# 512-column matmuls in place of 128-column ones in the idle stretches of TensorE

## The chip, the core and the metric

The kernel runs on one core of a Trainium2 chip. Its engines work side by side, each on its own list of instructions in order: TensorE (PE; its weight loads are listed apart, as PEld), VectorE (DVE), ScalarE (ACT), GpSimd (POOL) and SyncE (SP), which here only starts transfers. They wait for one another by semaphores. The metric is the device time of one execution in microseconds (us); of the kernel before it is 308.48 us, the median of three runs (307.95 to 309.0).

## The reference

Attention over selected chunks, then a gated feed-forward layer on its result, cut to what matters:

```python
B, H, S, D = 4, 8, 768, 64;  chunk, top_k = 32, 6
k_min, k_max = min and max of k over each chunk of 32 tokens
ub   = sum_d max(q * k_min, q * k_max)            # a bound for each query and chunk
ub   = where(causal by chunk, ub, -1e9)
sel  = the 6 chunks with the largest ub
attn = softmax(where(sel & causal, q @ k.T / sqrt(D), -1e9)) @ v
x    = attn, heads side by side                   # 3072 tokens x 512
xn   = x / sqrt(mean(x*x) + 1e-6) * rms_g
g    = xn @ w_gate                                # 512 -> 1536
out  = (silu(g) * (xn @ w_val)) @ w_out           # 1536 -> 512
```

Inputs and output are float32.

## The kernel before, in words

**Tiling.** The 768 tokens of each of the 4 batch entries are cut into 3 blocks of 256, 12 blocks in all, worked through in the list `ORDER`. A block has two groups `g` of four heads. For every block and group, `job` turns k and q so that the head's dimension lies on the partitions (DVE, L639), makes bfloat16 copies `kb` and `qb` (L646/L647), takes the chunks' minimum and maximum `kx` (DVE, L654) and lays them out in `BD`. `pick` multiplies them with q in float32 on PE (`upper`, L559), finds the sixth largest bound with DVE (`ubn`, `bar`, `top`, `mk`, `mt`, L580 to L611) and so makes the masks `mtd` and `mto`. Then come the scores with the masks added on PE (L717, L728), the exponential on ACT (L767), the causal triangle on POOL (L737), the product with v on PE (`values`, L793), and the division on DVE (L812). `norm` takes the root mean square (ACT, POOL), and turns the rows with PE (`turn`, L856).

`ffn` takes 512 columns of a gate product `wg` and of a value product `wv` in PSUM (16 matmuls of 128 columns each, or 8 of 256; L894), a tanh on ACT (L901), `tg` on DVE (L905), a copy `vs` of the value product on ACT (L913) and the product `hh` on POOL (L916); for the pairs in `DIRECT` the product is taken on DVE from PSUM (L909) and there is no copy. Then 24 matmuls of 512 columns (`project`, L926) for each 128 tokens, a copy out and a store. The first two blocks are in `SPLIT`: their feed-forward part runs in halves of 128 tokens, and part of their scores needs no mask.

**Weights.** `wg`, `wv` and `wo` are loaded in three thirds each, in nine transfers of 512 KB issued by POOL from 10.3 us on (wg0, wv0, wg1, wv1, wg2, wv2, wo0, wo1, wo2). A gate product of the second third of the hidden columns needs wg1 and wv1. By `HELD`, the k and v of the third block wait for wg0 and wv0, and those of the fourth for wo0.

**Order.** The whole order is laid down ahead by `Plan.run` when the program is built: each operation has an assumed duration, a priority `pri` (lower goes first), the operations it needs, and the buffers it takes. The planner picks, time step by time step, for each engine the operation that can start. Priorities come from due times: `due_ffn(i) = PACE * i` and `due_attn(i) = PACE * i - LEAD`. `MARGIN` is time that it adds to the expected landing of later loads. The chip doesn't follow the assumed times; it keeps the order on each engine, and the semaphores do the rest.

**Filler.** `fill` tells the planner what to do where PE would be idle for a while in its own times, from 1.6 to 60 us: it puts in matmuls whose result nobody reads (`keep_busy`, L991), into a free PSUM buffer `F`. Up to `cold` = 5.6 it reckons with twice `step` for each, after that with `step` = 0.0565 us:

```python
n = int(max(0.0, min(t1, cold) - t0) / (2 * step) + max(0.0, t1 - max(t0, cold)) / step)
...
TE.matmul(store["F"][slot][:, 0:P], ident[:], ident[:], start=True, stop=True)
```

Each of them is a weight load and a matmul in PE's list. There are 256 of them, all within the first 40 us.

Of the kernel before, what the change touches and what calls it, by code (L numbers as in the profile page):

```python
# [10 lines left out]
ALU = mybir.AluOpType  # L11
ACT = mybir.ActivationFunctionType
# [102 lines left out]
class Plan:  # L115
# [44 lines left out]
    def run(self, in_order=(), fill=None):  # L160
        left = {k: len(v) for k, v in self.readers.items()}
        last = {}
        slot = self.slot = {}
        head = {p: 0 for p in self.fifo}
        at = {e: 0.0 for e in self.HOP}
# [57 lines left out]
        while todo:  # L223
            best = None
            for e, c in cand.items():
                if not c:
                    continue
                rows = [(est(o, e), o) for o in c]
                rows = [(t, o) for t, o in rows if t is not None]
                if not rows:  # L230
                    continue
                t0 = max(at[e], min(t for t, o in rows))
                now = sorted(((t, o) for t, o in rows if t <= t0 + 1e-9),
                             key=lambda r: (r[1].pri, r[1].seq))
                t, o = now[0]
                if e in self.PATIENT:
                    soon = [r for r in rows if r[0] <= t0 + self.PATIENT[e]]
                    for t, o in now + sorted(soon, key=lambda r: (r[1].pri, r[1].seq)):
                        end = t + o.alts[e][0] - 0.1
                        if not any(t < r[0] < end and r[1].pri < o.pri - 10 for r in soon):  # L240
                            break
                    t0 = max(t0, t)
                if best is None or (t0, o.pri) < (best[0], best[1].pri):
                    best = (t0, o, e)
            if best is None:
                stuck = [o.name for c in cand.values() for o in c][:12]
                raise RuntimeError(f"no op can go on: {stuck}")
            t, o, e = best
            todo -= 1
            if e == "PE" and fill is not None:  # L250
                begin, cold, end, step, pool, fn = fill
                t0 = max(begin, at[e])
                f = sorted(x for x in self.free[pool] if x[0] + 0.055 <= t0)
                t1 = min(t, end) - (0.11 if o.mode != "full" else 0.03)
                n = int(max(0.0, min(t1, cold) - t0) / (2 * step) + max(0.0, t1 - max(t0, cold)) / step)
                if n > 0 and f:
                    w = Op("warm", "PE", t1 - t0, t1 - t0, lambda n=n, x=f[0][1]: fn(n, x), 0)
                    w.seq, w.start, w.mode = -1, t0, "full"
                    w.done = at[e] = t1
                    mode = "full"  # L260
                    order.append(w)
            for x in o.alts:
                cand[x].remove(o)
            o.eng = e
            o.occ, o.lat, o.fn = o.alts[e]
            if e == "PE" and mode is not None and mode != o.mode:
                t += 0.105
            if e == "PE":
                mode = o.mode
            o.start = t  # L270
            if e in port and shares(o, e):
                port[e] = (t, t + o.lat - 0.06)
            at[e] = t + o.occ
            o.done = t + o.lat
            if o.dma is not None:
                packets, cost, hw = o.dma
                rings.add(max(2.3, t + o.occ + (0.6 if hw else 1.4)), e, packets, cost, o)
                if hw:
                    at[e] = max(at[e], rings.room(e, t))
                if hw:  # L280
                    lanes.append(o)
            for key in o.takes:
                p = self.pool_of[key]
                if p in strict:
                    while head[p] < len(self.fifo[p]) and self.fifo[p][head[p]].start is not None:
                        head[p] += 1
                self.free[p].sort()
                slot[key] = self.free[p].pop(0)[1]
            for key in o.uses:
                last[key] = max(last.get(key, 0.0), o.done)  # L290
                left[key] -= 1
                if not left[key]:
                    self.free[self.pool_of[key]].append((last[key], slot[key]))
            order.append(o)
            for u in o.users:
                n_dep[u.seq] -= 1
                if not n_dep[u.seq]:
                    offer(u)
# [6 lines left out]
def kernel(  # L305
# [12 lines left out]
    P = nc.NUM_PARTITIONS  # L318
# [11 lines left out]
    NHT = DFF // P  # L330
    NTOK = B * S
    SCALE = 1.0 / (D ** 0.5)
    KH = NHT // 2
# [13 lines left out]
    def at(key):  # L347
        return store[plan.pool_of[key]][plan.slot[key]]
# [46 lines left out]
    ORDER = [(0, 0), (1, 0), (2, 0), (3, 0), (0, 1), (1, 1), (0, 2), (2, 1), (1, 2),  # L395
             (3, 1), (2, 2), (3, 2)]
    assert sorted(ORDER) == [(b, m) for b in range(B) for m in range(NBLK)]
    PACE, LEAD = 23.0, 70
    MARGIN = 3.0
    FIRST = 8  # L400
    SPLIT = {0, 1}
    APART = set()
    PACKED = {0, 1, 2}
    DIRECT = {(i, hp) for i in range(len(ORDER)) for hp in range(KH) if i >= 4 and hp % 2}

    def HALVES(i):
        return ((0,), (1,)) if i in SPLIT else ((0, 1),)
# [1 line left out]
    def due_attn(i):  # L409
        return PACE * i - LEAD  # L410
# [465 lines left out]
    def ffn(i, toks):  # L876
# [7 lines left out]
        for hp in range(KH):  # L884
            third = 3 * hp // KH
            gp, vp = ("gp", *U, hp), ("vp", *U, hp)
            th, vs, tg, hh = ("th", *U, hp), ("vs", *U, hp), ("tg", *U, hp), ("hh", *U, hp)
            pri = base + hp * 6 // KH
            for nm, p_, w in (("wg", gp, wg), ("wv", vp, wv)):
                def gate(p_=p_, w=w, hp=hp):  # L890
                    for n in range(K):
                        ht = K * hp + n
                        for g in range(NP):
                            TE.matmul(at(p_)[:, n * W:(n + 1) * W],  # L894
                                      w[:, g, ht * P:(ht + 1) * P], at(xT)[:, g, 0:W],
                                      start=(g == 0), stop=(g == NP - 1), skip_group_check=True)

                o = plan.op(f"{nm}{U}.{hp}", "PE", 0.873, 1.035, gate, pri,
                            reads=[xT, (nm, third)], writes=[p_], takes=[(p_, "F")])
                o.mode = "full"  # L900
            plan.op(f"tanh{U}.{hp}", "ACT", 0.48, 0.6, lambda th=th, gp=gp: SE.activation(  # L901
                out=at(th), in_=at(gp), func=ACT.Tanh, scale=0.5), pri - 20, reads=[gp], writes=[th],
                takes=[(th, "th")])
            plan.op(f"tg{U}.{hp}", "DVE", 0.6, 0.69, lambda th=th, gp=gp, tg=tg:
                    VE.scalar_tensor_tensor(  # L905
                        out=at(tg), in0=at(th), scalar=1.0, in1=at(gp), op0=ALU.add,
                        op1=ALU.mult), pri - 30, reads=[th, gp], writes=[tg], takes=[(tg, "tg")])
            if (i, hp) in DIRECT:
                plan.op(f"hh{U}.{hp}", "DVE", 0.6, 0.69, lambda tg=tg, vp=vp, hh=hh: VE.tensor_tensor(  # L909
                    out=at(hh), in0=at(tg), in1=at(vp), op=ALU.mult), pri - 30, reads=[tg, vp],  # L910
                    writes=[hh], takes=[(hh, "hh")])
                continue
            plan.op(f"vcopy{U}.{hp}", "ACT", 0.48, 0.6, lambda vs=vs, vp=vp: SE.activation(  # L913
                out=at(vs), in_=at(vp), func=ACT.Copy), pri + 0.1, reads=[vp],
                writes=[vs], takes=[(vs, "vs")])
            plan.op(f"hh{U}.{hp}", "POOL", 1.11, 1.16, lambda tg=tg, vs=vs, hh=hh: GE.tensor_tensor(  # L916
                out=at(hh), in0=at(tg), in1=at(vs), op=ALU.mult), pri - 10, reads=[tg, vs],
                writes=[hh], takes=[(hh, "hh")])
        for k_, s in enumerate(toks):
            op, ob = ("op", i, s), ("osb", i, s)  # L920
# [2 lines left out]
            def project(h0, h1, k_=k_, op=op):  # L923
                for ht in range(h0, h1):
# [8 lines left out]
                        writes=[op], takes=[(op, "F")])  # L933
            o.mode = "full"
            o = plan.op(f"project{i}.{s}+", "PE", 0.216 * K, 0.216 * K + 0.17,
                        lambda project=project: project(last, NHT), pri - 10,
                        reads=[("hh", *U, KH - 1), op], writes=[op])
            o.mode = "full"
            flex(f"out{i}.{s}", {
# [20 lines left out]
    for i in range(len(ORDER)):  # L960
# [12 lines left out]
            for j in jobs:  # L973
                next(j, None)
        for toks in HALVES(i):
            norm(i, toks, due_attn(i) + (7 if toks[-1] else -3))
        if i == 0:
            for n in range(3):
                load_w(n, -290 if n == 0 else -36 + n)
# [6 lines left out]
        for toks in HALVES(i):  # L986
            ffn(i, toks)

    def keep_busy(n, slot):
        for _ in range(n):  # L990
            TE.matmul(store["F"][slot][:, 0:P], ident[:], ident[:], start=True, stop=True)  # L991

    for o in plan.run(in_order=("kraw", "qraw", "vraw", "kT", "qT", "kb", "qb", "VX", "xsT", "xs", "hh", "xnat"),
                      fill=(1.6, 5.6, 60.0, 0.0565, "F", keep_busy)):
        o.fn()
    kernel.plan = plan
# [28 lines left out]
```

The softmax here doesn't subtract the row's maximum and nothing guards it: scores larger than these inputs give would overflow.

## Time and profile before

| | before |
|---|---|
| time, median of 3 | 308.48 us |
| span of the profiled execution | 307.3 us |
| PE busy from 0 to 8, 8 to 24, 24 to 50 us | 6.55 of 8, 15.16 of 16, 23.80 of 26 us |
| PE busy from 50 to 303 us | 249.29 of 253 us |
| fillers (L991) | 256, 20.03 us, the last at 39.2 us |
| mean granted TensorE clock | 0.987 |
| instructions fetched for PE (queue q8) | 39 packets, 0.64 MB |

Landing of the weights' last piece, by the trace's semaphore updates: wg0 18.91, wv0 21.45, wg1 25.45, wv1 29.70, wg2 33.10, wv2 36.42, wo0 39.82, wo1 42.86, wo2 46.37 us.

How to read it: an engine's busy time is the sum of its instructions in the stretch; the rest is idle. The granted clock is the share of full speed that the throttle let TensorE have. In the profile's chain of waits each piece of the span is put down to the instruction that the end waited for, and "issue" to time for which the records name no releaser. A group line gives source line, engine, operation and what it writes and reads. Queue q8 carries instructions only; q0 the weights; q1 and q10 the other loads and the stores.

### The profile page before, as it was taken

The numbers are of one execution on the slowest core, as the hardware profiler recorded it, in microseconds if no ns is written. First come the engines' busy times: TensorE is split into PE (matmuls) and PEld (weight loads), VectorE is DVE, ScalarE is ACT, GpSimd is POOL, SyncE is SP. The second block draws the span as 40 slices with busy tenths as digits, with TensorE's granted clock in tenths as the row PEclk, the third lists the DMA queues.
The fourth block names the chain that finished last, engine by engine and source line by source line (L and its number), as shares of the span: only waits on it lengthen the run. The fifth ranks groups of instructions, "written<-read, shape, count | busy, mean of one in ns | idle before, by whom it ended". The sixth has DMA issues, their size and how long they took to land.

```text
span 307.3 us, 11903 instructions
## 1 busy us (share of the span) xinstructions
PE 294.8 (96%) x4966; PEld 233.1 (76%) x4992; DVE 218.3 (71%) x560; ACT 210.4 (68%) x364; POOL 146.6 (48%) x266
## 2 busy tenths in 40 slices
PE   8897999998999999999999999999999999999994
PEld 8796999666867867876885876788588598688671
DVE  7994498865896898999999898269467245247250
ACT  3663786778986996966788777669478479565240
POOL 4783488656773694553656553235243034114130
PEclk9997899999999999999999999999999999999999
DMA  8999995575853434555763500100110010010101
GB/s 191 239 213 254 197 207 124 131 191 136 212 120 105 108 68 114 131 132 129 166 132 103 140 3 2 70 5 0 36 38 2 2 71 3 35 38 0 69 2 68
DMA packets 74838, 30.66 MB, mean 100 GB/s; under 512 B 65568, under 2 KB 70176, under 8 KB 74784
## 3 DMA queue, kind: packets, MB, share of 16 engines
q1 hardware_dynamic: 69184, 24.66, 32.9%
q0 software_dynamic: 4752, 4.72, 9.1%
q8 instruction: 39, 0.64, 0.9%
q10 hardware_dynamic: 848, 0.53, 0.6%
q14 instruction: 15, 0.12, 0.1%
HBM read 28.31 MB, written 6.29 MB: 113 GB/s over the span
## 4 chain that ended last, share of the span: by engine, by line
PE 88%; DVE 3%; issue 2%; ACT 2%; DMA 1%; POOL 1%; ACTq 0%; DVEq 0%
PE F L894 40%; PE F L926 19%; PE S L717 8%; PE F L793 7%; PE S L559 6%; PE F L991 3%; PE S L728 3%; PE F L856 2%; DMA qraw<-in_q_dram 1%; DVE kx L654 1%; DVE qT L639 1%; DVE tg L905 0%; POOL pt L737 0%; ACT junk L828 0%; ACT th L901 0%
## 5 line engine op out<-in xcount | busy, mean ns | idle before, releaser
L767 ACT ACTIVATE pt<-S 128x1024 bf16<-128x1024 f32 (+3 forms) x104 | 86.2, 861 | 23.5 <-PE S L728 23.0
L916 POOL TENSOR_TENSOR hh<-tg,vs 128x512 bf16<-128x512 bf16 x48 | 55.9, 1168 | 64.8 <-ACT vs L913 42.8
L894 PE MATMUL F<-xsT,wg 128*128 128x256 bf16 (+1 forms) x672 | 75.7, 260 | 0.5 <-DVE xnat L812 0.4
L894 PE MATMUL F<-xsT,wv 128*128 128x256 bf16 (+1 forms) x672 | 74.7, 257 | 0.0
L905 DVE SCALAR_TENSOR_TENSOR tg<-th,F 128x512 bf16<-128x512 bf16 x72 | 48.7, 680 | 35.8 <-ACT th L901 34.6
L926 PE MATMUL F<-wo,hh 128*128 128x512 bf16 x262 | 63.8, 379 | 1.9 <-issue 1.0
L894 PEld LDWEIGHTS <-wg 128*128 128x128 bf16 x672 | 57.4, 99 | 8.3 <-issue 0.9
L894 PEld LDWEIGHTS <-wv 128*128 128x128 bf16 x672 | 57.2, 98 | 7.5 <-issue 0.3
L901 ACT ACTIVATE th<-F 128x512 bf16<-128x512 f32 x72 | 43.0, 599 | 20.3 <-PE F L894 17.8
L737 POOL TENSOR_SCALAR_AFFINE_SELECT pt<-pt 128x512 bf16<-128x512 bf16 x48 | 31.1, 654 | 37.6 <-ACT pt L767 36.5
L926 PEld LDWEIGHTS <-hh 128*128 128x128 bf16 x288 | 26.4, 98 | 28.0
L913 ACT ACTIVATE vs<-F 128x512 bf16<-128x512 f32 x48 | 28.4, 600 | 9.3 <-PE F L894 8.4
L717 PE MATMUL S<-qb,kb 32*128 32x256 bf16 (+1 forms) x800 | 33.1, 254 | 0.7 <-DVE ubn L580 0.3
L654 DVE TENSOR_REDUCE kx<-kT 128x16 f32<-128x512 f32 x48 | 30.0, 668 | 0.0
L793 PE MATMUL F<-VX,pt 128*128 128x65 bf16 x672 | 27.1, 194 | 0.9 <-POOL kx L659 0.7
L793 PEld LDWEIGHTS <-pt 128*128 128x128 bf16 x672 | 24.1, 98 | 3.0 <-issue 1.4
L828 ACT ACTIVATE junk<-xnat 128x512 bf16<-128x512 bf16 x24 | 15.2, 633 | 13.1 <-DVE xnat L812 8.2
L717 PEld LDWEIGHTS <-kb 32*128 32x128 bf16 x800 | 13.8, 93 | 13.0 <-issue 11.9
L991 PE MATMUL F<-ident 128*128 128x128 bf16 x256 | 20.0, 244 | 1.9 <-POOL ident masks.py:199 1.4
L812 DVE TENSOR_TENSOR xnat<-F,rden 128x256 bf16<-128x256 f32 x48 | 20.1, 423 | 1.3
L728 PE MATMUL S<-mtd,chunkrow 32*128 32x128 bf16 (+2 forms) x384 | 20.5, 203 | 0.0
L728 PE MATMUL S<-mto,chunkrow 32*128 32x128 bf16 (+2 forms) x384 | 19.9, 203 | 0.0
(60 smaller groups left out, 357.3 us busy)
## 6 DMA issues: line engine op xcount, KB each, us to landing
vraw<-in_v_dram SPq DMA_DIRECT2D x24, 256.0 KB, 4.4
out_dram<-osb SPq DMA_DIRECT2D x24, 256.0 KB, 2.2
kraw<-in_k_dram SPq DMA_DIRECT2D x72, 64.0 KB, 2.5
qraw<-in_q_dram SPq DMA_DIRECT2D x72, 64.0 KB, 2.2
wg<-in_moe_w_gate_dram POOLq DMA_DIRECT2D x3, 512.0 KB, 12.3
wv<-in_moe_w_val_dram POOLq DMA_DIRECT2D x3, 512.0 KB, 15.8
wo<-in_moe_w_out_dram POOLq DMA_DIRECT2D x3, 512.0 KB, 22.7
kraw<-in_k_dram SPq DMA_DIRECT2D x10, 128.0 KB, 4.3
```

Source lines behind the costliest of these rows:

```text
L654: plan.op(f"ext{n}{J}", "DVE", 0.585, 0.67, lambda n=n, op=op: VE.tensor_reduce(out=at(kx)[:, n], in_=at(kT).rearrange("p h (c t) -> p h c ...
L717: TE.matmul(s[a // 2][:, a % 2, c0:c0 + q1 - q0], kbt[r, t, ks], qbt[r, t, q0:q1], start=(t == 0), stop=(t == 1 and not mask), skip_group_ ...
L728: TE.matmul(o, chunkrow[r, BLK * kg + P * e:BLK * kg + P * (e + 1)], mv, start=False, stop=(d == 1), skip_group_check=True)
L737: GE.affine_select(out=d, in_=d, compare_op=ALU.is_ge, fill=0.0, base=0, pattern=[[0, 4], [1, P]], channel_multiplier=-1)
L767: lambda pt=pt, hs=hs, c0=c0, c1=c1, x=sc[hp]: SE.activation(out=at(pt)[:, hs, c0:c1], in_=at(x)[:, :, c0:c1], func=ACT.Exp, scale=SCALE), ...
L793: TE.matmul(o[:, a, :], p_[:, a, off:off + P], vt[:, e, a, :], start=(kb_ == 0 and a == 0), stop=(kb_ == nkb - 1 and a == 3), skip_group_c ...
L894: TE.matmul(at(p_)[:, n * W:(n + 1) * W], w[:, g, ht * P:(ht + 1) * P], at(xT)[:, g, 0:W], start=(g == 0), stop=(g == NP - 1), skip_group_ ...
L901: plan.op(f"tanh{U}.{hp}", "ACT", 0.48, 0.6, lambda th=th, gp=gp: SE.activation(out=at(th), in_=at(gp), func=ACT.Tanh, scale=0.5), pri - 2 ...
L905: VE.scalar_tensor_tensor(out=at(tg), in0=at(th), scalar=1.0, in1=at(gp), op0=ALU.add, op1=ALU.mult), pri - 30, reads=[th, gp], writes=[tg ...
L916: plan.op(f"hh{U}.{hp}", "POOL", 1.11, 1.16, lambda tg=tg, vs=vs, hh=hh: GE.tensor_tensor(out=at(hh), in0=at(tg), in1=at(vs), op=ALU.mult) ...
L926: TE.matmul(at(op)[:], at(("hh", *U, ht // K))[:, o:o + P], wo[:, ht, :], start=(ht == 0), stop=(ht == NHT - 1))
L991: TE.matmul(store["F"][slot][:, 0:P], ident[:], ident[:], start=True, stop=True)
```

## The change

From 5.6 us of the planner's time on, a gap on PE is filled with matmuls of 512 columns (the moving operand is 512 columns of `chunkrow`), one for each 0.216 us of the gap, in place of one of 128 columns for each 0.0565 us. Before 5.6 us the filler stays as it was. The same work time then takes a quarter of the instructions. With it, constants of the planner are set anew: `PACE`, `LEAD`, `MARGIN`, the set `APART` (blocks in which the choice of chunks is done for one group of heads after the other), the set `DIRECT` (now from the block at place 5 on), and some priorities.

```diff
             if e == "PE" and fill is not None:
-                begin, cold, end, step, pool, fn = fill
+                begin, cold, end, step, wide, pool, fn = fill
...
                 n = int(max(0.0, min(t1, cold) - t0) / (2 * step) + max(0.0, t1 - max(t0, cold)) / step)
+                if t0 >= cold:
+                    n = int((t1 - t0) / wide)
                 if n > 0 and f:
-                    w = Op("warm", "PE", t1 - t0, t1 - t0, lambda n=n, x=f[0][1]: fn(n, x), 0)
+                    w = Op("warm", "PE", t1 - t0, t1 - t0,
+                           lambda n=n, x=f[0][1], c=t0 >= cold: fn(n, x, c), 0)
...
-    PACE, LEAD = 23.0, 70
-    MARGIN = 3.0
+    PACE, LEAD = 23.5, 73
+    MARGIN = 2.0
     FIRST = 8
     SPLIT = {0, 1}
-    APART = set()
+    APART = {0, 1}
     PACKED = {0, 1, 2}
-    DIRECT = {(i, hp) for i in range(len(ORDER)) for hp in range(KH) if i >= 4 and hp % 2}
+    DIRECT = {(i, hp) for i in range(len(ORDER)) for hp in range(KH) if i >= 5 and hp % 2}
...
-                out=at(th), in_=at(gp), func=ACT.Tanh, scale=0.5), pri - 20, reads=[gp], writes=[th],
+                out=at(th), in_=at(gp), func=ACT.Tanh, scale=0.5), pri - 0, reads=[gp], writes=[th],
...
-                        op1=ALU.mult), pri - 30, reads=[th, gp], writes=[tg], takes=[(tg, "tg")])
+                        op1=ALU.mult), pri - 40, reads=[th, gp], writes=[tg], takes=[(tg, "tg")])
...
-                    out=at(hh), in0=at(tg), in1=at(vp), op=ALU.mult), pri - 30, reads=[tg, vp],
+                    out=at(hh), in0=at(tg), in1=at(vp), op=ALU.mult), pri - 40, reads=[tg, vp],
...
-                out=at(hh), in0=at(tg), in1=at(vs), op=ALU.mult), pri - 10, reads=[tg, vs],
+                out=at(hh), in0=at(tg), in1=at(vs), op=ALU.mult), pri - 40, reads=[tg, vs],
...
-                        lambda project=project: project(last, NHT), pri - 10,
+                        lambda project=project: project(last, NHT), pri - 20,
...
-            norm(i, toks, due_attn(i) + (7 if toks[-1] else -3))
+            norm(i, toks, due_attn(i) + (7 if toks[-1] else -12))
...
-    def keep_busy(n, slot):
+    def keep_busy(n, slot, wide):
         for _ in range(n):
-            TE.matmul(store["F"][slot][:, 0:P], ident[:], ident[:], start=True, stop=True)
+            x = chunkrow[:, 0:512] if wide else ident[:]
+            TE.matmul(store["F"][slot][:, 0:x.shape[1]], ident[:], x, start=True, stop=True)
...
-                      fill=(1.6, 5.6, 60.0, 0.0565, "F", keep_busy)):
+                      fill=(1.6, 5.6, 60.0, 0.0565, 0.216, "F", keep_busy)):
```

## The prediction

> **What bounds the kernel now.** I read the shares per engine first, then the chain of waits, then the same chain enlarged around its largest gap, then the busy time by stretch.
>
> ```profile
> PE 294.8 (96%) x4966; PEld 233.1 (76%) x4992; DVE 218.3 (71%) x560; ACT 210.4 (68%) x364; POOL 146.6 (48%) x266
> ...
> PEclk9997899999999999999999999999999999999999
> ...
> PE 88%; DVE 3%; issue 2%; ACT 2%; DMA 1%; POOL 1%; ACTq 0%; DVEq 0%
> ```
>
> TensorE (PE) is the bound, and the chain runs through it for 88% of the span. Two things are out of line: "issue" (time in which the engine waited for nothing that the profile shows) and a dip of the clock in slices 4 and 5. The enlarged chain (start, length, what) puts both in one place:
>
> ```profile
> 23.77 0.77 PE S L559 x39
> 24.54 2.05 issue
> 26.58 0.87 PE S L559 x24
> 27.45 0.33 PE F L991 x2
> 27.78 1.71 PE F L894 x16
> 29.49 0.33 PE S L717 x7
> 29.82 2.78 PE F L991 x25
> ```
>
> In the middle of one `upper` group PE stops for 2.05 us with all operands there; afterwards 16 gate matmuls take 1.71 us against 0.89 us elsewhere in the chain, and 25 fillers 2.78 us, 111 ns each. The stretches name the rate (columns: PE, PEld, DVE, ACT, POOL busy, granted clock, DMA):
>
> ```profile
> 22.90:26.30 3.40, 1.64 (x61) 1.42 (x56) 1.46 (x6) 1.74 (x5) 2.65 (x6) 1.00 1.16 274
> 26.30:29.70 3.40, 3.12 (x50) 2.71 (x50) 1.83 (x10) 0.18 (x1) 0.33 (x1) 0.50 1.17 252
> 29.70:33.10 3.40, 3.40 (x42) 3.16 (x38) 0.69 (x1) 1.61 (x5) 1.20 (x2) 0.50 1.22 198
> ...
> 40.00:303.00 263.00, 259.14 (x4236) 200.00 (x4259) 189.11 (x493) 187.19 (x314) 123.19 (x195) 1.00 0.33 81
> ```
>
> After a stretch in which PE was busy for 1.64 of 3.40 us it gets half the clock for two such stretches (26.32 to 33.15 in the clock records). The other engines wait for it meanwhile. From 40 to 303 us PE idles only 3.9 us in all, so what is lost before 35 us is carried to the end.
>
> The cause of the 2.05 us is in the DMA records. The queue that carries only instructions (q8) moves 39 packets of 16 KB; PE's trace has about 10,000 records, so one packet is 256 instructions. Counting PE's instructions from the start (a float32 matmul of `upper` stands for four records), the gap at 24.54 falls near instruction 953, a gap of 0.44 us at 13.84 near 444, and between them, at 698, a hiccup of 0.1 us at 20.2: a spacing of 256. Each packet starts about when PE enters the block before the one it brings. From 50 us on that is mostly within 1 us. Between 10 and 44 us, while the 16 DMA engines carry the weights (DMA share 1.2), it is 2.7 to 4.4 us later, takes 1.0 us, and PE goes on 1.5 to 1.65 us after it ends. So **a block of 256 instructions that PE gets through in less than 5 to 7 us, mostly 6.2, stalls it** there.
>
> **What the Trainium skill says.** "Runtime: NRT & Kernel Launch", Instruction fetch mechanics, has instructions refilled in 16 KiB blocks of 256 by the sequencer's own DMA queue; the 39 packets agree. It calls a crossing "mostly hidden"; between 10 and 44 us it is not. "DMA: Bandwidth & Descriptors", Issuing engines are not separate DMA queues, says that all DMAs share the 16 engines and interleave, which fits the late packets. "TensorE: Matmul & The Clock Gate", What's actually happening, gives half clock or full clock in free-running windows of about 3.4 us; the 0.50 stretches and their 6.83 us agree. Its section Wait — 56ns, not 53.3ns? prices 512 columns at 215.7 ns; in this trace 19 projection matmuls of 512 columns take 4.26 us, 224 ns each, and 16 fillers of 128 columns 0.89 us, 56 ns.
>
> **The change part by part.**
>
> Fillers. Before: 256 of 128 columns, 86 of them ahead of the first scores. After: the same 86, then 36 of 512 columns in place of 170. Warm PE time falls from 170 x 56 = 9.5 us to 36 x 0.216 = 7.8 us, and PE reads 2 x 134 = 268 fewer instructions, one whole block, before 40 us. The matmul time alone is worth little, since PE would wait for masks and weights in its place. What matters is which work straddles a block.
>
> Blocks, walked with the after-program's instruction list. Block 444 is now entered at the end of the first masked scores of block 0, about 16.4 us, long after its packet (14.3): the 0.44 us goes. Block 698 is then due at 16.4 + 6.2 = 22.6 us and lies in the `upper` of the second block, which PE reaches at about 23.4 (weights wv0 land at 21.45, then wv 0.89, scores 0.2, three fillers 0.65, half the group): no stall. Block 953 is due at 23.4 + 6.2 to 6.7, say 29.9 us. PE's work between the two is half an `upper` 0.45, two fillers 0.43, gate 0.89, turn 0.23, the other half 0.49, filler 0.22, gate 0.89, scores 0.43 = 4.0 us, so PE is there early again, at 27.4 us or, with the wait for wg1 below, 28.5. But the instruction behind the boundary is the gate's wv of hidden third 1, whose weights landed at 29.70 in the trace before (its landing semaphore), and the first of these gates needs wg1, landed at 25.45, some 1.1 us after PE gets there (24.3). **The weights now set what the instructions set before.** Block 1209 is due at 29.9 + 6.2 = 36.1; PE's work from 953 is 4 gate groups at 0.89, three values 0.26, a turn 0.23, scores 0.43, two fillers 0.43 = 5.4 us, to 35.3: a wait of 0.8 us. From there to the `upper` of ORDER's third block: 10 groups (8.9 us) and a turn, 45.2 us. In the trace before that `upper` starts at 50.26 with one gate group more behind it (19 against 18): 45.2 + 0.9 = 46.1. **Gain 4.1 us**, if the clock holds.
>
> APART {0, 1}: the pick of two blocks is cut in two; DVE has 7 instructions more in all and three products fewer, so ten short ones more, some 0.6 us around 15 us and again around 25 us by the 0.06 to 0.3 us of these rows. PE is then filling or waiting for wg0 (landed 18.91): nothing on the path. Half of the second `upper` can start before the other half's kx.
>
> DIRECT from block 5 instead of 4: three products leave DVE (0.68 us each) for ACT (0.60) and POOL (1.17). POOL is busy 48%: nothing.
>
> PACE, LEAD, MARGIN and priorities only reorder; the work is the same, and PE's last 24 projections and the output tail (303 to 307.3 us) stay. Behind a newly waiting PE instruction stands all of PE's queue, then ACT's tanh and DVE's tg. I price this at 0 with -1 to +3 us as bounds: of 3.9 us idle from 40 to 303 us part could go, and a poor order could double it.
>
> Loads after the weights: wo lands by 46.37, its first use moves from 53.1 to about 49; kraw of the fourth block is held until wo0 (39.8) and was first read at 54.8. Both have slack.
>
> **Rivals.**
> - *The clock drops again.* PE would idle about 1.2 us in each of two 3.4 us windows, 35%. The trace shows a drop at 52% idle and none at about 20% (0.69 us at 76 us): undecided. Half clock from 26.3 costs some 2 us by 33.1, of which the 0.8 us wait gives back part: gain 2.8. From 29.7 it costs up to 3.4: gain 1.5. Time 306.3.
> - *All of it comes back, and some of the later idle.* 2.05 + 0.44 of stall and half of 6.83 us of clock is 5.9 us; the landing of wv third 1 speaks against it. Time 302.5.
> - *The gain is given back later.* DVE is busy 9.7 to 9.9 of 10 us between 120 and 170 us, so it may not follow a PE that is 4 us ahead. Against: over 50 to 303 it has 29% free. Time 308.4.
> - *Slower.* The new order starves PE somewhere in 250 us: 3 us of new waits plus two half-clock windows, with a stall kept. 308.5 + 2 = 310.5. Against: the list after 50 us differs mainly in where gates and projections stand around the same attention steps.
>
> **How the numbers follow.** Forecast 0.36 (304.4), clock drop 0.20 (306.3), all back 0.17 (302.5), given back 0.11 (308.4), slower 0.16 (310.5). The forecast is 308.48 - 4.1 = 304.4. Faster by over 0.3% (under 307.55): 0.36 + 0.20 + 0.17 = 0.73; same 0.11; slower 0.16. The range runs from 301.8, the second rival with its -1 us of later idle, to 308.6, and leaves out the slower case and little else.
>
> **What would show it.** Right: no "issue" in the middle of an `upper`; clock 1.0 throughout; PE waits named DMA wg or wv, or issue, of about 1 us at 24 to 30 us; third block's `upper` at about 45 us. Wrong in size: a 0.50 clock stretch after 26 us. Wrong in kind: PE idle from 50 to 303 us well above 3.9 us, or the same 2 us stall at another boundary with half clock behind it.

## The result and the profile after

The changed kernel takes **305.83 us** (median of 4 runs, 305.58 to 306.20), the kernel before in the same comparison 308.22 us (307.92 to 309.0). The ratio is 0.992, with a 95% interval of 0.9897 to 0.9942: 2.4 us faster, 1.4 us above the forecast. The ratios of this document leave out executions over 1.5% above the fastest of their kernel, of which there are two, both of `together_bare`. The profiled spans are 304.1 and 307.3 us; of their difference of 3.2 us some 0.75 is the profiled execution of before, which has two half-clock stretches and took 308.97 us, that much above the median.

Lines of the changed kernel's profile that answer to those shown of before: shares of the engines, the granted clock by slice, the chain of waits by engine. Its line numbers are 3 higher (L897 is L894 of before, L562 is L559).

```profile
PE 290.7 (96%) x4830; PEld 224.7 (74%) x4858; DVE 218.9 (72%) x565; ACT 217.5 (72%) x382; POOL 147.5 (49%) x267
...
PEclk9999999999999999999999999999999999999999
...
PE 76%; DVE 5%; ACT 2%; issue 1%
```

The last line covers less than its counterpart of before: here the profile follows the chain back to 44.0 us only, and the four shares add up to 84%. The dip of the clock is gone. PE is still the bound, busy 96% of a span that is 3.2 us shorter: the shares alone tell nothing of where the time came from. The timeline of PE does (start, length, what; in brackets the idle time just before it and what ended it):

```profile
24.35 0.50 PE L562 MATMUL S<-qT,BD 64*64 64x32 f32 x16 [0.83 <-ACT pt L770]
...
28.40 1.05 PE L897 MATMUL F<-xsT,wg 128*128 128x128 bf16 x16 [0.30 <-DVE xsT L872]
...
29.81 0.34 PE L897 MATMUL F<-xsT,wv 128*128 128x128 bf16 x3
31.20 0.89 PE L897 MATMUL F<-xsT,wv 128*128 128x128 bf16 x13 [1.05 <-issue]
...
37.67 2.51 PE L897 MATMUL F<-xsT,wg 128*128 128x128 bf16 x42 [0.34 <-issue]
```

No `upper` is cut by a stall of instruction supply any more. Two such stalls remain, and both lie at 256-instruction boundaries: after three of 16 `wv` matmuls at 30.15 (the fourth is about instruction 956) and at 37.33 (about 1212). The packet for the first starts at 28.77 and ends at 29.70 us in the DMA records; PE goes on 1.5 us after that. The second `upper` starts late for another reason, a wait of 0.83 us for an exponential (`pt`) on ACT.

A mark that all the profiles share is the first `upper` of `ORDER`'s third block. It starts at 50.26 us before (first line) and at 47.65 us after (second line):

```profile
50.26 0.43 PE L559 MATMUL S<-qT,BD 64*64 64x32 f32 x16
47.65 0.43 PE L562 MATMUL S<-qT,BD 64*64 64x32 f32 x16
```

One gate group (0.89 us) more lies ahead of it before, so the early gain at equal work is 1.72 us. From that mark to the end of the span it is 257.04 us before, 257.93 with that group, and 256.45 after: another 1.48 us is gained in the 250 us behind it. The prediction had 4.1 and 0. Both measured figures are from single executions, and the early one holds the 0.75 us by which that execution of before was slower than its median: of the 2.4 us between the medians some 0.9 us would be early (an estimate, 2.4 less 1.48).

### The profile page after: what moved, and what is told of

The parts are those of the page before. It is cut to its first block, busy times and chain, and to the rows that moved or that the text cites. A ratio compares the mean times of both kernels' runs of the same rounds, so it can differ in the third digit from the quotient of the medians.

```text
span 304.1 us, 11660 instructions
## 1 busy us (share of the span) xinstructions
PE 290.7 (96%) x4830; PEld 224.7 (74%) x4858; DVE 218.9 (72%) x565; ACT 217.5 (72%) x382; POOL 147.5 (49%) x267
## 4 chain that ended last, share of the span: by engine, by line
PE 76%; DVE 5%; ACT 2%; issue 1%
PE F L897 34%; PE F L929 20%; PE S L720 7%; PE F L796 6%; PE S L562 5%; PE S L731 3%; PE F L859 1%; DVE kx L657 1%; DVE tg L908 1%; ACT pt L770 1%; DVE xnat L815 1%; ACT junk L831 0%; DVE qT L642 0%; DVE m L597 0%; ACT th L904 0%
## 5 line engine op out<-in xcount | busy, mean ns | idle before, releaser
L919 POOL TENSOR_TENSOR hh<-tg,vs 128x512 bf16<-128x512 bf16 x51 | 59.3, 1165 | 83.7 <-ACT vs L916 63.0
L897 PE MATMUL F<-xsT,wv 128*128 128x256 bf16 (+1 forms) x672 | 75.1, 257 | 1.7 <-issue 1.1
L897 PE MATMUL F<-xsT,wg 128*128 128x256 bf16 (+1 forms) x672 | 74.8, 257 | 1.1 <-DVE xnat L815 0.5
L897 PEld LDWEIGHTS <-wv 128*128 128x128 bf16 x672 | 56.7, 98 | 9.0 <-issue 2.4
L897 PEld LDWEIGHTS <-wg 128*128 128x128 bf16 x672 | 56.7, 98 | 8.9 <-issue 1.4
L916 ACT ACTIVATE vs<-F 128x512 bf16<-128x512 f32 x51 | 30.7, 601 | 6.8 <-PE F L897 5.9
L945 DVE TENSOR_SCALAR osb<-F 128x512 f32<-128x512 f32 x14 | 9.5, 688 | 17.5 <-PE F L929 17.5
```

The source lines that it names most:

```text
L897: TE.matmul(at(p_)[:, n * W:(n + 1) * W], w[:, g, ht * P:(ht + 1) * P], at(xT)[:, g, 0:W], start=(g == 0), stop=(g == NP - 1), skip_group_ ...
```

## Experiments

The theory after the first comparison: narrow fillers use up blocks of 256 instructions faster than they arrive, so PE's pace before 40 us is set by the blocks, and wide fillers free it; the new order of the other work is a separate effect. The rivals: the gain is the clock; or the gain is the new constants, with the fillers beside the point.

The medians of before in the same comparisons were 307.97 to 308.73 us; each ratio is to its own.

| kernel | time, us | ratio to before (95%) |
|---|---|---|
| changed kernel, second time (`after_again`) | 305.66 | 0.9921 (0.9903 to 0.9940) |
| `fill_only` | 308.77 | 1.0015 (0.9999 to 1.0030) |
| `tune_only` | 307.14 | 0.9953 (0.9935 to 0.9970) |
| `fill_frozen` | 305.29 | 0.9913 (0.9892 to 0.9934) |
| `bare_frozen` | 305.10 | 0.9897 (0.9877 to 0.9918) |
| `shift` | 310.44 | 1.0078 (1.0056 to 1.0099) |
| `exp_first` | 305.04 | 0.9889 (0.9854 to 0.9925) |
| `exp_first_again` | 304.78 | 0.9886 (0.9866 to 0.9907) |
| `no_wide` | 305.12 | 0.9903 (0.9871 to 0.9934) |
| `together` | 306.40 | 0.9940 (0.9919 to 0.9960) |
| `together_bare` | 307.20 | 0.9962 (0.9941 to 0.9982) |
| `all_bare` | 307.49 | 0.9980 (0.9966 to 0.9995) |

Nobody reads what a filler computes, so the kernels with fewer fillers compute the same outputs. The second profile of the changed kernel has the same waits as the first (1.0 us for `pt`, stalls of 1.2 and 0.3 us), and its mark is at 47.83 us.

### The two halves of the change, as the source has them

`fill_only` is before with the wide fillers' lines of the diff alone; `tune_only` is the changed kernel with those lines undone, so with its constants and 243 narrow fillers.

> The kernel before with the wide fillers alone; PACE, LEAD, MARGIN, APART, DIRECT and the priorities stay. Theory (blocks of 256 instructions that come late set the loss before 35 us, and the fillers' instruction count is what counts): PE enters block 444 at about 16.9 and block 698 at about 23 us, no stall at either; behind 698 it reaches the gate that needs wv1 before its landing (29.5) and waits for the weights, not for instructions; the second block's upper runs through. 304.5 to 306.5, the upper end if the wait for wv1 (up to 2 us in one window) brings the half clock back. Rival (the retuned constants did it, the fillers are decoration): within 0.5 us of before.

> The changed kernel with the narrow fillers of before (243 of 128 columns), all retuned constants kept. Theory of the blocks: block 444 falls into fillers at about 14 us (stall of some 0.4), block 698 into scores at about 19 us with its packet usable at about 20.2 (stall of 1 to 1.5), block 953 into the fillers behind half of the second upper at about 25 with its packet usable at 26.5 to 27 (stall of 1.5), and the half clock after it: 307 to 309, no better than before. Rival (the retuning did it): 305.5 to 306.5 as the changed kernel.

`tune_only` came at the low end of what was expected, 307.14 us, without the half clock that was expected with it. Its profile has the stalls of instruction supply, at other places than before (the four longest waits of PE from 8 to 50 us: total, times, longest):

```profile
PE F L793 <- issue: 1.2, 1, 1.2
PE S L728 <- issue: 1.1, 1, 1.1
PE F L991 <- issue: 0.8, 1, 0.8
PE F L894 <- issue: 0.7, 1, 0.7
```

These are 3.8 us against 2.5 before. It is faster than before all the same, since from the third block's `upper` (48.76 us, with as many gate groups ahead as in the changed kernel) to the end it needs 256.34 us: the later gain comes with the constants and not with the fillers. The traces of all engines show the same order of work here as in the changed kernel, fillers apart. So this run also compares narrow with wide fillers in that order: the wide ones reach the mark 1.1 us earlier in the profiles, and the times are 305.66 to 305.83 against 307.14 us.

`fill_only` missed: 308.77 us in place of 304.5 to 306.5. In the same stretch its waits are of other kinds:

```profile
PE F L897 <- DMA wv<-in_moe_w_val_dram: 1.7, 2, 1.0
PE F L897 <- DMA wg<-in_moe_w_gate_dram: 1.4, 2, 0.8
PE S L720 <- ACT qb L649: 1.3, 1, 1.3
PE F L897 <- issue: 0.6, 1, 0.6
```

Only 0.6 us of a supply stall is left. But the planner counts a filler as work, and with fillers of another length it laid down another order for all engines here (with the changed constants, in `tune_only`, it did not). This order lost later what was gained early. From the mark (47.78 us) to the end it is 260.3 us, with 17 gate groups ahead of the mark in place of 19; at equal work that is 0.7 us gained ahead of it and 1.5 us lost behind. In that profile the weights also landed later (wv0 at 22.91, wv1 at 31.26 us) than before (21.45 and 29.70). So the edit that looks like "the fillers alone" is not that, and the next ones hold the order fixed.

### The fillers alone, in before's order

`fill_frozen` lets the planner of before work as it did, and changes only what a run of fillers emits: 45 wide ones for the 170 narrow ones that follow the first 86. `bare_frozen` emits nothing for those 170.

```diff
     def keep_busy(n, slot):
-        for _ in range(n):
-            TE.matmul(store["F"][slot][:, 0:P], ident[:], ident[:], start=True, stop=True)
+        if n > 80:
+            for _ in range(n):
+                TE.matmul(store["F"][slot][:, 0:P], ident[:], ident[:], start=True, stop=True)
+            return
+        for _ in range(int(n * 0.0565 / 0.216 + 0.5)):
+            TE.matmul(store["F"][slot][:], ident[:], chunkrow[:, 0:512], start=True, stop=True)
```

and for `bare_frozen`:

```diff
     def keep_busy(n, slot):
-        for _ in range(n):
+        for _ in range(n if n > 80 else 0):
```

> The kernel before with its order kept to the last instruction, only that each run of n narrow fillers behind the first 86 is replaced by n x 0.0565 / 0.216 wide ones (45 in all). Theory: two shares make up the change, the early one from fewer instructions in front of the late blocks, and a later one (0.6 us around 75 us, 0.9 us around 177 us) from the new order. Then this kernel keeps before's waits at 74, 76 and 176 us, has no 2 us stall inside the second upper and no half clock, and gains the early share alone: 1 to 2 us, 306.3 to 307.4. Rival (the fill has no part in it, as the run with wide fillers and a re-laid order seemed to say): 308.2 to 308.8.

> The kernel before with its order kept, and all 170 fillers behind the first 86 left out; it computes the same. If the fillers earn their place by the clock: half clock in most windows from 12 to 34 us and 308.5 to 310. If the instruction blocks cost more than the clock saves (PE waits for masks and weights there anyway): no stall named issue before 40 us, half clock in some windows, and 306 to 307.5, as good as wide fillers.

`fill_frozen` gains more than expected: 305.29 against 307.97 us, **2.7 us, as much as the whole change**. Its PE timeline has waits for the weights where the stalls had been, and one short stall; the last line is the mark:

```profile
25.20 1.07 PE L894 MATMUL F<-xsT,wg 128*128 128x128 bf16 x16 [0.39 <-DMA wg<-in_moe_w_gate_dram]
...
29.41 1.07 PE L894 MATMUL F<-xsT,wv 128*128 128x128 bf16 x16 [0.66 <-DMA wv<-in_moe_w_val_dram]
...
36.41 0.56 PE L894 MATMUL F<-xsT,wg 128*128 128x128 bf16 x7 [0.60 <-issue]
...
46.55 0.43 PE L559 MATMUL S<-qT,BD 64*64 64x32 f32 x16
```

The third block's `upper`, with the same work ahead of it as before, starts at 46.55 us in place of 50.26, 3.7 us earlier, and from there to the end it is 257.05 us, as in before (257.04). So in this order the early gain is carried to the end and neither grows nor shrinks. The 3.7 us is 1.0 us more than the timed 2.7, since the profiled execution of before was 1.0 us slower than the median of this comparison. The weights are not far ahead of the instructions here: the wait for wv ends at 29.41 us, and PE crosses the next block boundary, 19 instructions on, at 29.94, 1.5 us behind the packet's end and 6.45 us after it entered the block before. Those are the distances of the stalled crossings, so had the weights come earlier, PE would probably have stood at the boundary in their place; no run separates the two.

`bare_frozen` is as fast, 305.10 us. Leaving the 170 narrow fillers out is worth 2.9 us. They were put in to keep the clock up, and without them the clock does fall (columns as in the stretches of before: busy PE, PEld, DVE, ACT, POOL, then the clock):

```profile
12.90:23.10 10.20, 7.25 (x143) 6.21 (x136) 8.27 (x22) 6.21 (x13) 8.99 (x16) 0.50 1.25 212
23.10:29.90 6.80, 4.81 (x155) 3.96 (x153) 4.80 (x19) 4.79 (x15) 4.85 (x10) 1.00 1.18 261
29.90:33.40 3.50, 3.50 (x41) 3.50 (x39) 0.83 (x4) 2.08 (x6) 0.64 (x1) 0.51 1.21 194
```

The clock records show half clock for 13.65 us in all (12.91 to 23.15, 29.98 to 33.39), and the third block's `upper` still starts at 47.62 us, 2.6 us earlier than before. In the first of these stretches PE is idle for 2.95 of 10.2 us even at half clock; its longest waits before 50 us are for `xs` (1.7 us in two), the mask `mtd` (1.7) and `BD` (1.0). This execution was the slowest of the five, though: 306.31 us at a mean clock of 0.975, where the others took 304.73 to 305.11 us at 0.981 to 0.983, which is about 10 us of half clock in all (an estimate from the mean clock and the span).

The clock is not what the change gains. Before loses to `fill_frozen` without a dip too: of the 95 timed runs of before beside these experiments, 32 had a mean clock of 0.998 or more, and their median is 308.16 us. One half-clock stretch of 3.41 us would bring the mean clock to 0.994 (an estimate from the span). The wide fillers do better than none by 1.07 us at the mark of the two profiles, but the medians can't be told apart.

### More instructions, the same work

If it is the count of instructions that stalls PE, more of them at the same PE time must move the stalls. `shift` takes before and replaces 64 of its first 86 fillers, long ahead of the stalls, with two of 64 columns each: 128 instructions more (64 weight loads and 64 matmuls).

```diff
+        for k_ in range(n):
+            if n > 80 and k_ >= n - 64:
+                for _ in range(2):
+                    TE.matmul(store["F"][slot][0:64, 0:64], ident[:, 0:64], ident[:, 0:64], start=True, stop=True)
+                continue
```

> The kernel before with 64 of its first 86 fillers each replaced by two of 64 columns: the same PE time at the start, 128 instructions more, all else in the same order. Theory of the blocks: every boundary moves 128 instructions forward in the work. No gap at the old places (inside the fillers behind the first values, inside the second upper); new gaps named issue in the first masked scores near 17 us (about 1 us), in the second block's first scores near 23 us (about 1 us), and in the 25 fillers behind them near 28 us (about 2 us). Rival (the gap at 24.5 hangs on what upper waits for, or on a fixed time): it stays inside the second upper. Time 307.5 to 309.5 under both; the places decide.

It is slower by 0.78% (310.44 us), and in its PE timeline the stalls stand elsewhere:

```profile
16.44 0.22 PE L717 MATMUL S<-qb,kb 32*128 32x128 bf16 x3
19.33 0.27 PE L717 MATMUL S<-qb,kb 32*128 32x128 bf16 x5 [2.67 <-issue]
...
29.71 0.95 PE L995 MATMUL F<-ident 128*128 128x128 bf16 x14
32.24 0.79 PE L995 MATMUL F<-ident 128*128 128x128 bf16 x11 [1.57 <-issue]
```

One is now in the middle of the first masked scores (about instruction 700), one in the middle of the 25 fillers that ran in one piece before (about 1212), and the second `upper`, where before stood still for 2.05 us, has none. No data dependence changed, and a stall followed the instruction number. The places were those expected but for two: at about 956 PE arrived after the packet, and there was no gap, and one block behind the fillers, at 38.43 us, stood a third stall, of 1.28 us, that was not named. The sizes were not as expected (2.67 us where 1 was). 128 instructions more cost 2.5 us here (310.44 against 307.97), of which 0.29 us may be work: the first scores start at 9.04 us in place of 8.75.

### What the new order costs early

In the changed kernel the exponential that the second `upper` waits for stands on ACT behind the square of `norm`, which itself waits for DVE's `xnat` (timeline of ACT):

```profile
23.22 0.63 ACT L831 ACTIVATE junk<-xnat 128x512 bf16<-128x512 bf16 x1 [1.51 <-DVE xnat L815]
23.75 0.19 ACT L831 ACTIVATION_READ_ACCUMULATOR junk<-xnat 128x1 f32 x1
23.84 0.36 ACT L770 ACTIVATE pt<-S 128x256 bf16<-128x256 f32 x1
```

The scores that it reads had been ready at 22.8 us. `exp_first` takes the laid-down order and moves this one instruction behind the exponential:

```diff
+    late = order.pop(names.index("square01"))
+    names = [o.name for o in order]
+    order.insert(names.index("exp(1, 0, 1)0a0") + 1, late)
```

> The changed kernel with one instruction moved: on ACT the square of block 0's second half goes behind the exponential that frees the score buffer which the second block's upper takes. PE's order is the same. Theory (the forecast missed because upper waited 0.83 us for that exponential, so block 698 was entered at 24.5 and the packet of 953 came at 31.2): upper starts at about 23.5, the stall at 953 ends at about 30.3, and the end comes 0.5 to 0.9 us earlier: 305.0 to 305.3. Rival (the stall at 953 hangs on the DMA engines alone, not on when PE enters the block before): the stall ends at 31.2 again, 305.8.

The time, 305.04 us, is as expected. Its profile fell on an execution with late weights (wv0 at 23.71, wv1 at 32.25 us, that execution 307.69 us), so it doesn't show the place. A second run of the same kernel does:

> The changed kernel with one ScalarE instruction moved, a second time, for a trace in which the weights land as early as in the changed kernel's own (wv0 by 21 us, wv1 by 29.5 us). If the late exponential behind the square is what makes the second `upper` late: the 0.83 us wait for `pt` ahead of it is gone, the 1.05 us stall of instruction supply inside the wv gate at 30 us shrinks to 0.3 us or turns into a wait for wv1, and the time is 305.0 to 305.4 us. Rival, only the landing of the weights counts: another wait stands in the same place, the stall stays at 1 us and the time is 305.7 to 305.9, that of the changed kernel.

304.78 us, a little better than expected, but the stall of supply did the opposite of what was expected (timeline of PE):

```profile
21.87 1.07 PE L897 MATMUL F<-xsT,wv 128*128 128x128 bf16 x16 [0.51 <-DMA wv<-in_moe_w_val_dram]
...
23.85 0.43 PE L562 MATMUL S<-qT,BD 64*64 64x32 f32 x16
...
28.51 0.34 PE L897 MATMUL F<-xsT,wv 128*128 128x128 bf16 x3
30.45 0.89 PE L897 MATMUL F<-xsT,wv 128*128 128x128 bf16 x13 [1.60 <-issue]
```

The wait for `pt` is gone, and PE gets to the boundary 1.3 us earlier, at 28.85 us, and stands there for 1.60 us, longer than the 1.05 us of the changed kernel. It still goes on 0.75 us earlier (30.45 against 31.20). The block before that boundary, number 700, lies at the start of this `upper`. It is entered at 23.97 in place of 24.47 us, its successor's packet starts at 27.85 in place of 28.77, and PE goes on 6.5 us after the entry (6.7 in the changed kernel). So here **the entry into one block sets the time of the next**, and the length of a stall says only how early PE came. The third block's `upper` starts at 46.90 us, 0.75 us earlier than in the changed kernel, and from there to the end it is 256.5 us as there. The intervals of its ratio and of the changed kernel's overlap by a little only (0.9897 to 0.9907), and the two profiles agree with a difference.

`no_wide` leaves out the 36 wide fillers of the changed kernel and keeps its order:

> The changed kernel with its 36 wide fillers left out, order of all else unchanged (the 86 narrow ones at the start stay). If the fillers hold the clock: PE is idle for over half of a window between 9 and 17 us, half clock from about 13 on for two windows or more, and 306.5 to 308. If PE's wait for masks and weights hides that, and the clock matters only from 20 us on: 305.5 to 306.0. Under the theory of the blocks alone the stall at 953 moves by 72 instructions to the values behind the third-1 gates and is no longer than 1 us.

305.12 us: the medians show no worth of the wide fillers in this order either. But the six executions spread from 304.42 to 307.94 us, where those of `after_again` lie within 0.45 us, and the shortest has the highest mean clock (0.985), the longest, which is the profiled one, the lowest (0.972). In that one the weights came late too (wg1 at 27.58 us, with a wait of 1.8 us for it), so the clock isn't shown to be the cause.

### Was it the choice of chunks in two parts?

Since the order of before with wide fillers is 2 us ahead of the changed kernel at 50 us, I suspected `APART = {0, 1}`, which cuts the choice of the first two blocks in two. `together` is the changed kernel with `APART = set()`; `together_bare` is the same without wide fillers, and `all_bare` without any filler.

> The changed kernel with APART empty again, so that the choice of chunks of the first two blocks is done for both groups at once, as before; wide fillers and the other constants stay. Theory (the early share is 3.7 us with the order of before and 1.7 us with the changed one, because the second block's upper waits for an exponential and for BD and each later packet comes late by as much; the later share of 1.5 us belongs to PACE, LEAD and the priorities): early part as with before's order and wide fillers, later part as changed, 303.8 to 304.8. Rival (the later order hangs on APART as well, or the early loss has another cause): 305.3 to 306.

> The same, with the wide fillers left out and the 86 narrow ones at the start kept. Theory (the fillers cost instructions and the clock that they hold is hardly needed, since TensorE waits for masks and weights until 30 us): within 0.5 us of the kernel with wide fillers, half clock in three to five windows of 3.4 us. Rival (the half clock costs): 1 to 2 us slower.

> The same with no filler at all, the first 86 left out too. The first scores and the first upper then run at half clock, and each step of the chain of scores, exponential, upper, masks before 20 us is longer by the PE time in it, 0.13 to 0.97 us. If that chain is on the path: 0.5 to 1.5 us slower than with the first 86 alone. If the weights' landing (wg0 at 18.4 to 19.3) hides it: the same.

306.40 us: the suspicion fell, and its rival's range was exceeded a little. As in `fill_only` the planner laid down a new order, with its own waits (DMA wv 1.2, DMA wg 0.9, `issue` 0.7 us), so this doesn't say what `APART` costs by itself. `together_bare` scatters from 305.0 to 310.6 us: its runs with a mean clock of 0.983 lie near 305.1, those at 0.964 to 0.971 between 307.9 and 310.6. In this order the lower clock does go with a longer time; whether as its cause, or because both follow from late weights, isn't settled. `all_bare` at 307.49 shows no measurable worth of the first 86 fillers over `together_bare`. Against `together` with all its fillers it is 1.1 us slower, and the intervals of the two ratios don't touch, so in this order fillers are worth something. That is little for what it lost: its clock records begin at 23.24 us, and until then its matmuls are as slow as those of before at half clock (1.89 us for a gate group, 1.91 there; timeline of PE, with a later group for comparison):

```profile
19.64 1.89 PE L897 MATMUL F<-xsT,wg 128*128 128x128 bf16 x16 [1.34 <-DMA wg<-in_moe_w_gate_dram]
...
26.09 1.07 PE L897 MATMUL F<-xsT,wg 128*128 128x128 bf16 x16
```

The mean clock of this run, 0.994, counts the time ahead of the first record as full clock, so it says nothing of this stretch.

## Why the prediction was right, and where it was not

**The bound and the cause of the stalls: right.** A block of 256 instructions that PE gets through faster than the next one comes, in 5.9 to 7.1 us by the stalled crossings of these profiles, stalls it before 40 us. `shift` and the frozen orders show it from both sides. "Mostly hidden", as the Trainium skill has it in "Runtime: NRT & Kernel Launch", Instruction fetch mechanics, holds in these profiles behind 50 us and not in the first 40, where single crossings cost 0.3 to 2.7 us.

**Fillers: right in kind, and nearly in size, but for another order.** The walk through the blocks gave 4.1 us. With before's order kept, the wide fillers gave 3.7 us at the third block's `upper` in the profile and 2.7 us in the timed runs. "The weights now set what the instructions set before" holds there by the waits (0.39 us for wg, 0.66 for wv), though instructions were due at almost the same time, and not in the changed kernel, where instruction supply was still the last to come at both boundaries.

**PACE, LEAD and priorities "at 0": the step that failed, twice, with opposite signs.** In the changed kernel the walk ran late from its first step on:

| mark, us | predicted | measured | added here |
|---|---|---|---|
| block entered in the second `upper` | 23.4 | 24.47 | 1.07, of it 0.83 the wait for `pt` |
| block in the `wv` gate | 29.9 | 31.20 | 0.23 |
| next block | 36.1 | 37.67 | 0.27 |
| third block's `upper` | 45.2 | 47.65 | 0.88, of it 0.23 for `vs` and 0.41 for `tg` |

The sum is 2.45 us, and 1.72 us is left of the early gain. The 0.83 us is a wait that I did not price: I named what stands behind PE's instructions, but not what stands ahead of ACT's exponential. `exp_first_again` shows it to be worth 0.75 us. The rest of the early loss is spread over small waits, and which constant brought it isn't settled. Later the new order gains 1.48 us, whatever the fillers: from the mark to the end the profiles of the changed kernel's order (`tune_only`, `no_wide`, and `exp_first` twice, one instruction moved) have 256.3 to 256.5 us, and those of before's order (both frozen ones, `shift`) 257.0 to 257.1. What brings it could not be placed. Of before's waits near 75 us the 0.69 us for `kx` is gone; the 0.44 us for `xnat` stands (0.45). PE's idle time from 50 to 300 us is 3.0 us after (28.96 + 88.79 + 129.24 us busy of 250) and 3.7 us before (28.42 + 89.25 + 128.63), but that is no safe guide, for `fill_frozen`, with before's order and before's time behind the mark, shows 2.3.

So the forecast's nearness to the time is partly two errors of about 2.4 and 1.5 us that cancel. Together they make 1.0 us of the miss of 1.4. The rest is a slip of the sum: the gain of 4.1 us was reckoned from the profiled execution of before, which took 308.97 us, but was taken off the median, 308.48.

**The clock: right that it holds, oversized in worth.** The clock records of the changed kernel's profile show no half clock from 7.18 us, where they begin, to the end. I had reckoned half of 6.83 us, 3.4 us, for it in the rivals. Of the 95 timed runs of before beside these experiments, 32 had a mean clock of 0.998 or more and a median of 308.16 us, 40 had 0.992 to 0.997 and 308.08 us, and 23 had less and 308.80 us: some 0.7 us. Why it is so little isn't shown for before. In `bare_frozen` PE was idle for 2.95 of 10.2 us even at half clock, so there slow matmuls filled time in which it would have waited.

**DIRECT, the loads of wo, the tail at nothing: not contradicted.** None was tried alone; no wait on wo or on the moved products shows among PE's waits from 50 us on.

**The rivals.** "The clock drops again" did not happen, and yet its time, 306.3 us, is nearer to the 305.83 measured than the forecast is: right number, wrong reason, luck. "All back and some later idle" was right that something is gained later. "Given back later" is wrong in sign for this order, and right for that of `fill_only`, whose later loss has no shown cause.

**Two slips that changed nothing.** DVE is busy 9.5 to 9.9 of 10 us between 120 and 170 us, not 9.7 to 9.9, as 150 to 160 us has 9.48. And the lower end of the range, 302.5 less 1 us of later idle, is 301.5 and not 301.8.

## What to carry to other kernels

Work that only fills an engine's idle time still uses instructions: where the profile shows `issue` on an engine with its operands ready, count instructions between such gaps before looking for a wait, and fill with few long instructions or with none. When a planner lays out the whole program, an edit of one cost moves everything; to learn what one part does, keep the order and change only what is emitted (`fill_frozen`, not `fill_only`). Don't price a lower clock by its length alone: where PE waits for something else it may cost little. And judge a stall by the time at which it ends, not by its length.

## What the runs showed of the hardware, unexpected

Blocks of instructions arrive in a rhythm of their own while the DMA engines are full (DMA share 1.1 to 1.2): at the crossings at 30 and 37 us of the changed kernel and of `exp_first_again` the packet starts 3.9 to 4.3 us after PE enters the block before, takes 0.9 to 1.1 us, and PE goes on 1.3 to 1.5 us after its end, 6.5 to 6.7 us in all. The stalled crossings of `shift` and `tune_only` have 5.9 to 7.1 us. No run changed the load of the DMA engines, so it isn't shown that this load is what makes the packets late.

The same nine weight transfers landed at different times in different executions (wv0 from 20.5 to 23.7 us, wv1 from 27.5 to 32.3 us). In one and the same kernel this turned a stall of instruction supply into a wait for DMA: `exp_first` waits 1.9 us for wv, which landed at 32.25 us, where `exp_first_again`, with wv at 29.87, stands 1.60 us for instructions.

And about 10 us of half clock (an estimate) cost nothing that the median of `bare_frozen` could tell, and in its profile PE was idle for 2.95 of 10.2 us even at half clock; the execution with 13.65 us was 1.2 us slower than the median, and whether by the clock isn't settled.
